# Attention, then a Gelu MLP, on one core: the first product of the MLP by seven block products from the fifth tile on, and high halves split by ScalarE

## Chip, cores and metric

One NeuronCore of a Trainium2 chip runs the whole program. The metric is the device time of one execution in microseconds (us); lower is better. Engines are named as the profile names them: PE is TensorE (PEld its weight loads), DVE is VectorE, ACT is ScalarE, POOL is GpSimd, SP issues DMAs.

## What is computed

```python
# q, k, v: 8 batches x 8 heads x 576 x 64, float32
scores = q @ k.T / sqrt(64)                      # causal, window of 128, ALiBi bias
attn   = exp(scores - max) / (sum + 1e-9)
x      = (attn @ v)   reshaped to 4608 x 512     # heads side by side
h      = x @ w_in                                # 512 -> 2048
out    = (0.5 * h * (1 + erf(h / sqrt(2)))) @ w_out   # 2048 -> 512
```

## The kernel before

The 4608 rows of x are cut into nine tiles of 512 tokens (t = 0 to 8). A batch has 576 tokens, so the attention of batch b fills the rest of tile b and the start of tile b + 1. Heads are worked in pairs; a pair of one batch is a *unit*, four units a batch.

Numbers of float32 precision are kept as two float16 halves: a *high part*, the value times a power of two, rounded, and a *low part*, what rounding left (`low_part`, L145, one VectorE instruction that reads the value and the high part). A product of two such numbers is three float16 matmuls: high by high, low by high, high by low. Batch 0 and half of tile 0 are in plain float32.

Tile by tile, from t = 1 on, the loop at L767 does 32 steps. Steps 0 to 15 are `mlp_in` (L588): 12 matmuls of 512 columns for one 128-wide slice of h, then Gelu by ScalarE out of PSUM into a float32 tile (L618), the high part of g by POOL (L619), the low part by VectorE (L620, a line of the helper L146). Steps 16 to 31 are `mlp_out` (L638): 12 matmuls of 512 columns each, and after every fourth step an eviction (`ob`, L661 by ScalarE or L663 by VectorE) and a store. Beside tile t stand the units of batch b = t + 1: `scores` (matmuls L410, scaled and biased into SBUF by VectorE, L432), `softmax` (row maxima L502, exp by ScalarE L505, z, the high part of e by ScalarE for b < 3 and by POOL from batch 3 on (L512, L514), the low part by VectorE, a transpose by DMA), and `weigh` (matmuls L554; the result goes to x by ScalarE L567 and VectorE). Their steps are in a table: scores at 2, 11, 16, 21, weigh at 12, 20, 25, 30 (other ones for t = 1). Once a tile, `split_v` and `split_qk` (L328, L350) measure and split the next batch's v, q and k in whole, 2560 and 2304 elements a partition.

PSUM has four banks for the MLP ("mm") and four for attention ("att"). x has two buffers, the float32 rooms "ob" three; each weight slice of w_in stays in SBUF, split into halves (`wi`). One e tile, `e_main`, serves all units. A scheduler orders the instructions of each engine from the order of the code, priorities and its own estimates; on the chip each engine keeps that order.

## Time and profile before

| | |
|---|---|
| median of 3 runs | 950.54 us (947.49 to 952.1) |
| the profiled execution | 956.14 us, of which its span (first to last instruction) is 954.3 |
| mean granted TensorE clock | 0.984 |
| busy in the span | PE 920.4, DVE 626.1, ACT 493.4, POOL 214.5 us |
| start of tile 2, 4, 7, 8 | 288.26, 492.50, 784.79, 867.67 us |
| last matmul ends | 950.56 us |

A group of instructions reads: line, engine, operation, out <- in, shapes, count | busy us, mean ns of one | idle time of the engine before them and who ended it. A row of the windows gives a stretch of the span, its length, the busy time of each engine with its number of instructions, the granted clock, the share of the DMA engines and GB/s. Matmuls overlap, so the mean of one (381 ns) is longer than the distance from one to the next. The kernel is compiled to lines of its own; line numbers below are those of the kernel before, unless they are said to be of the changed one.

### The profile page before, as it was taken

What the parts mean: (1) busy time and instruction counts of PE and PEld (TensorE: products, weight loads), DVE (VectorE), ACT (ScalarE), POOL (GpSimd) and SP (SyncE); (2) the same over time, 40 slices, a digit from 0 to 9 for tenths busy, and PEclk for the clock granted to TensorE, in tenths of its full rate; (3) what the DMA queues carried; (4) which work ended last, traced back from release to release, by engine and by line L of the source; (5) the groups of instructions that cost most, each with busy time, mean ns of one, the idle gap of its engine ahead of it and who ended that gap; (6) DMA issues with size and microseconds to landing.
All of it is one profiled execution on the core that took longest, in us unless ns stands there. A gap on an engine that the chain in (4) does not pass through costs nothing.

```text
span 954.3 us, 17680 instructions
## 1 busy us (share of the span) xinstructions
PE 920.4 (96%) x7068; PEld 448.8 (47%) x7068; DVE 626.1 (66%) x1270; ACT 493.4 (52%) x1071; POOL 214.5 (22%) x444
## 2 busy tenths in 40 slices
PE   7979999889999899999999999999999999999998
PEld 3554444544544444444544454444544454444443
DVE  6799989689786877497768876777566722201200
ACT  5978967767653664366525653564366313101200
POOL 1010000023001542053314430353044312201200
PEclk9889999799999999999999999999999999999999
DMA  9517433961473226522472346144312430000000
GB/s 313 211 65 264 179 105 94 208 191 29 98 176 99 50 58 144 148 46 55 77 201 46 56 94 178 52 77 94 73 30 50 92 75 1 1 23 23 1 12 33
DMA packets 172450, 91.18 MB, mean 96 GB/s; under 512 B 132560, under 2 KB 153168, under 8 KB 172240
## 3 DMA queue, kind: packets, MB, share of 16 engines
q1 hardware_dynamic: 172368, 90.06, 37.7%
q8 instruction: 55, 0.90, 0.4%
q14 instruction: 27, 0.22, 0.1%
HBM read 46.53 MB, written 9.44 MB: 59 GB/s over the span
## 4 chain that ended last, share of the span: by engine, by line
PE 54%; DMA 2%; DVE 2%; ACT 2%; issue 1%; SPq 0%; POOL 0%; DVEq 0%
PE o L653 26%; PE h L595 22%; PE av L554 3%; PE sc L410 2%; DMA v<-vp 1%; DMA q<-qp 1%; DVE stv L214 1%; DMA et<-e_main 1%; ACT vbuf L332 1%; DVE vbuf L146 0%; ACT s L505 0%; DVE kbuf L146 0%; ACT L618 0%; ACT L505 0%; SPq L305 0%
## 5 line engine op out<-in xcount | busy, mean ns | idle before, releaser
L595 PE MATMUL h<-x,wi 128*128 128x512 f16 x1728 | 385.0, 381 | 6.6 <-ACT g L618 3.0
L653 PE MATMUL o<-wo,g 128*128 128x512 f16 x1224 | 276.4, 379 | 0.2 <-DVE wo L146 0.2
L595 PEld LDWEIGHTS <-wi 128*128 128x128 f16 x1728 | 166.8, 98 | 209.2 <-issue 12.3
L653 PEld LDWEIGHTS <-g 128*128 128x128 f16 x1632 | 155.0, 98 | 186.6 <-issue 2.3
L146 DVE SCALAR_TENSOR_TENSOR g<-g,sg,g 128x512 f16<-128x512 f32 (+1 forms) x144 | 114.1, 805 | 92.7 <-POOL g L619 91.5
L619 POOL TENSOR_SCALAR g<-g,sg 128x512 f16<-128x512 f32 x128 | 100.4, 788 | 316.7 <-ACT g L618 312.4
L505 ACT ACTIVATE s<-s,nmax 128x192 f32<-128x192 f32 x252 | 111.2, 442 | 103.2 <-DVE nmax L502 103.0
L618 ACT ACTIVATE g<-h,gs 128x512 f32<-128x512 f32 x128 | 85.9, 687 | 135.8 <-PE h L595 111.0
L146 DVE SCALAR_TENSOR_TENSOR e_main<-s,z,e_main 128x192 f16<-128x192 f32 x252 | 107.3, 468 | 15.0 <-POOL e_main L514 10.2
L514 POOL TENSOR_SCALAR e_main<-s,z 128x192 f16<-128x192 f32 x180 | 87.1, 503 | 84.9 <-ACT s L505 29.3
L653 PE MATMUL o<-wo_first,g 128*128 128x512 f16 x408 | 94.6, 382 | 2.8 <-DMA wo_first<-wo 2.8
L410 PE MATMUL sc<-kbuf,qbuf 64*64 64x192 f16 (+1 forms) x1656 | 75.6, 264 | 10.8 <-DMA kbuf<-kp 4.5
L432 DVE SCALAR_TENSOR_TENSOR s<-sc,cs,bias_h 128x384 f32<-128x384 f32 x112 | 63.7, 606 | 14.3 <-PE sc L410 14.1
L567 ACT ACTIVATE x<-av,cx 128x448 f16<-128x448 f32 (+6 forms) x52 | 23.7, 474 | 72.8 <-PE av L554 72.6
L437 POOL MEMSET s<- 64x128 f32 (+1 forms) x112 | 19.2, 172 | 185.8 <-DVE s L432 167.3
L502 DVE TENSOR_REDUCE nmax<-s 128x5 f32<-128x960 f32 (+1 forms) x56 | 58.4, 1044 | 2.1
L661 ACT ACTIVATE ob<-o,so 128x512 f32<-128x512 f32 x17 | 11.5, 678 | 91.2 <-PE o L653 91.1
L410 PEld LDWEIGHTS <-qbuf 64*64 64x64 f16 x1512 | 36.1, 106 | 43.0 <-issue 40.2
L663 DVE TENSOR_SCALAR ob<-o,so 128x512 f32<-128x512 f32 x17 | 12.6, 744 | 60.0 <-PE o L653 60.0
L554 PEld LDWEIGHTS <-vbuf 128*64 128x64 f16 x1680 | 43.3, 115 | 12.4 <-issue 11.5
L554 PE MATMUL av<-et,vbuf 128*64 128x128 f16 (+1 forms) x1680 | 46.4, 216 | 2.6 <-DMA et<-e_main 2.6
L505 ACT ACTIVATION_READ_ACCUMULATOR s<-s,nmax 128x1 f32 x252 | 47.1, 187 | 0.0
(139 smaller groups left out, 737.8 us busy)
## 6 DMA issues: line engine op xcount, KB each, us to landing
v<-vp SPq DMA_DIRECT2D x32, 320.0 KB, 5.1
out<-ob SPq DMA_DIRECT2D x36, 256.0 KB, 2.1
raw<-w_in SPq DMA_DIRECT2D x8, 1024.0 KB, 14.2
raw<-w_out SPq DMA_DIRECT2D x8, 1024.0 KB, 5.3
q<-qp SPq DMA_DIRECT2D x7, 1152.0 KB, 6.2
k<-kp SPq DMA_DIRECT2D x7, 1152.0 KB, 7.1
qbuf<-qp SPq DMA_DIRECT2D x4, 288.0 KB, 5.1
kbuf<-kp SPq DMA_DIRECT2D x4, 288.0 KB, 5.5
```

The costliest lines, as they stand in the source:

```text
L146: nc.vector.scalar_tensor_tensor(out=dst, in0=src, scalar=scale, in1=high, op0=ALU.mult, op1=ALU.subtract)
L410: nc.tensor.matmul(ps[bank][o, n, 0:W], a, m, start=(i == 0), stop=(i == len(terms) - 1 and b > 0), skip_group_check=True,)
L432: nc.vector.scalar_tensor_tensor(out=s[:, bank[0] : bank[0] + k, :], in0=ps[bank][:, 0:k, 0:W], scalar=cs, in1=bias.broadcast_to([P, k, W] ...
L502: nc.vector.tensor_reduce(out=nmax[:, r], in_=s[:, r], axis=AX.X, op=ALU.max, negate=True)
L505: nc.scalar.activation(s[:, i, :], s[:, i, :], AF.Exp, bias=nmax[:, i : i + 1], accum_out=z[:, i : i + 1])
L514: nc.gpsimd.tensor_scalar(e[:, i, 0, c], s[:, i], z[:, i : i + 1], 1.0, op0=ALU.mult, op1=ALU.mult)
L554: nc.tensor.matmul(av[r, (j - blocks[0]) * QB : (j - blocks[0] + len(js)) * QB], v32s[b][:, hp, kb, r] if b < EXACT else vbuf[:, vi, hp, k ...
L567: nc.scalar.activation(x[:, 0], av[:, :n], AF.Copy, scale=c)
L595: nc.tensor.matmul(ph, wi[n][:, a, cc, k * P : (k + 1) * P], x[:, cc, b, :], start=(i == 0), stop=(i == 3 * NCC - 1),)
L618: nc.scalar.activation(g32, ph, AF.Gelu, scale=gsc[t, n])
L619: nc.gpsimd.tensor_scalar(g[:, r, 0], g32, gsg[t, n], 1.0, op0=ALU.mult, op1=ALU.mult)
L653: nc.tensor.matmul(o, both[:, a, c], wo[n][:, b, k, :], start=(fc == first and i == 0), stop=(fc == last and i == 2),)
```

## The change

1. **Seven products.** For tiles 4 to 8 (`FAST = 4`), `mlp_in` is replaced by a class `Seven`. For a quarter d of the 2048 columns of h (512 columns), x and w_in are taken as 2 x 2 blocks (halves of the tokens by alternate 128-row slices of the 512, and halves of the columns by those slices), and the block product is formed from seven products in place of eight, after Strassen and Winograd. A product is 12 matmuls of 256 columns, two slices of 256 side by side in one PSUM bank. Two banks are held a quarter, u and v. The products gather in them, and partial results are copied out (s1, s2, s3, by ScalarE) and added to v by VectorE. Each of the four results then has Gelu, its high part (ScalarE) and its low part (VectorE).

```python
def add(self, ps, w, m, first):
    n = 0
    for k in range(2):
        for i in range(2):
            for a, b in ((0, 0), (1, 0), (0, 1)):
                nc.tensor.matmul(
                    ps[:, k * HT : (k + 1) * HT], w(a, i)[:, k * P : (k + 1) * P], m(b, i),
                    start=first and n == 0, stop=True, skip_group_check=True,
                )
                n += 1

def out(self, hi, tok, src, room=None):
    ...
    room = src if room is None else room
    nc.scalar.activation(room, src, AF.Gelu, scale=gsc[t, 2 * d])
    ...
    nc.scalar.activation(g[:, :, 0], v, AF.Copy, scale=gsg[t, 2 * d])
    low_part(g[:, :, 1], v, gsg[t, 2 * d], g[:, :, 0])

p1: u  = lo0 . x1           ; s1 = copy(u)
p2: v  = lo1 . x2           ; s1 = v + s1 ; out(s1)
p6: u += T2 . S2            ; s2 = copy(u)
p5: v  = hi0 . S1
p7: u += T3 . S3            ; s3 = copy(u) ; s3 = v + s3 ; out(s3)
p4: u += T4 . x2'           ; out(u)
p3: v += hi1 . S4           ; s2 = v + s2 ; out(s2)
```

The last seven lines are the seven methods in short. `seven_steps` puts them in the order p1 p2 p6 p5 p7 for the first quarter, p1 p2 p4' p6 p3' p5 p7 for the next ones (' is of the quarter before), 13 steps of two products; the last p4 and p3 stand in the first steps of `mlp_out`. The tile then has 29 steps.

2. **Sums of weights**, `sums_of_weights`, beside tiles 2 and 3 (steps 4, 8, 12 and 16): eight times two VectorE sums of 512 elements, four of 256, a high part of 1024 by ScalarE and a low part by VectorE, and four stores to DRAM. T1 takes the place of weights in SBUF; T2, T3 and T4 are streamed back, 256 KB for a quarter and a tile (60 loads in all).

3. **Sums of x**, `sums_of_x`, twice for each of tiles 4 to 8, when the units that fill them have been weighed: VectorE sums of 1024 and four times 256, a high part by ScalarE, a low part by VectorE.

4. **High parts by ScalarE** everywhere: POOL's two instructions are gone.

```diff
-                if st.b < 3:
-                    nc.scalar.activation(e[:, i, 0, c], s[:, i], AF.Copy, scale=z[:, i : i + 1])
-                    continue
-                nc.gpsimd.tensor_scalar(e[:, i, 0, c], s[:, i], z[:, i : i + 1], 1.0, op0=ALU.mult, op1=ALU.mult)
+                nc.scalar.activation(e[:, i, 0, c], s[:, i], AF.Copy, scale=z[:, i : i + 1])
...
-        nc.gpsimd.tensor_scalar(g[:, r, 0], g32, gsg[t, n], 1.0, op0=ALU.mult, op1=ALU.mult)
+        nc.scalar.activation(g[:, r, 0], g32, AF.Copy, scale=gsg[t, n])
```

5. **q and k from batch 4 on** come pair by pair, twice: `load_pair` and `measure` for the maxima, then `load_pair` and `split_pair` (576 elements a partition) before the scores. Batches 3 on hold two pairs' halves in the space of four. v, q and k of a batch get their scales together (`scales`).

6. **The table of steps.** A fast tile runs scores of units 1, 2 and 3 at steps 4, 8 and 15, of unit 0 of the next batch at 22, weigh at 14, 19, 22, 25. Softmax of units 1 and 2 is held back to step 14, behind the seven products, with a gate. Unit 0 of batch 5 moves into tile 3 (step 25). Row maxima (`maxima`) are taken before the exps of the whole unit.

```diff
-    SCORES_AT, WEIGH_AT = (2, 11, 16, 21), (12, 20, 25, 30)
+    AT = ((8, 14, 18, 22), (17, 22, 26, 30)), ((2, 11, 16, 21), (12, 20, 25, 30)), ((4, 8, 15), (14, 19, 22, 25))
```

7. Buffers: one tile `ldbuf` with two halves takes the place of the rotating "ld" buffers; the sums of x, the streams and two rooms for s2 lie in it from tile 4 on. Weights of w_in share a scale in pairs of slices. A few powers of two follow.

What the order becomes, at three places. TensorE, the first product of tile 8, before: two slices of h follow each other, each in a bank of its own (h8_0, h8_1).

```order
L595 MATMUL h8_0_10073<-x8_8835,wi0_679 128x512
L595 LDWEIGHTS wi0_679
L595 MATMUL h8_0_10073<-x8_8835,wi0_679 128x512
L595 LDWEIGHTS wi0_679
L595 MATMUL h8_1_10091<-x8_8835,wi0_679 128x512 [waits Activation_49]
```

And now: the end of p7 and the start of p4 of the first quarter, both in bank u8_0, where p4 waits for ScalarE's copy of p7's result.

```order
L816 MATMUL u8_0_10947<-ldbuf_77 128x256
L816 LDWEIGHTS ldbuf_77 [waits DMAHW7_49]
L816 MATMUL u8_0_10947<-x8_9756,ldbuf_77 128x256 [waits Activation_49]
L816 LDWEIGHTS ldbuf_77
L816 MATMUL u8_0_10947<-x8_9756,ldbuf_77 128x256
```

The matmuls are 256 columns wide, and the next one in the order needs the bank of the last.

ScalarE at the same place, before: one Gelu after the other, each from the next bank (g32 is the float32 room, h8_n the bank).

```order
L618 ACTIVATE g32_8_0_10087<-h8_0_10073,gs8_0_10067 128x512 [waits DMAHW6_49,PE_49,Activation_49]
L618 ACTIVATE g32_8_1_10104<-h8_1_10091,gs8_0_10067 128x512 [waits DVE_49,DMAHW7_49,PE_49,Pool_49]
L618 ACTIVATE g32_8_2_10121<-h8_2_10108,gs8_0_10067 128x512 [waits DMAHW0_49,PE_49,Activation_49]
L618 ACTIVATE g32_8_3_10138<-h8_3_10125,gs8_0_10067 128x512 [waits DVE_49,PE_49]
L618 ACTIVATE g32_8_4_10156<-h8_4_10142,gs8_0_10067 128x512 [waits DVE_49,PE_49]
```

And now: copies (s1, s3, s2 in ldbuf), Gelus and high parts (g8) of two quarters in turn.

```order
L837 COPY s18_0_10960<-u8_0_10947 128x512 [waits DMAHW1_49,PE_49,Activation_49]
L827 ACTIVATE s18_0_10960<-s18_0_10960,gs8_10937 128x512 [waits DVE_49]
L830 ACTIVATE g8_0_10943<-s18_0_10960,sg8_10938 128x2x256 [waits Activation_49]
L848 COPY ldbuf_77<-u8_0_10947 128x512 [waits PE_49]
L856 COPY s38_0_11017<-u8_0_10947 128x512 [waits DMAHW2_49,PE_49]
L837 COPY s18_1_11037<-u8_1_11024 128x512 [waits DMAHW3_49]
L827 ACTIVATE s38_0_11017<-s38_0_11017,gs8_10937 128x512 [waits DVE_49]
L827 ACTIVATE s18_1_11037<-s18_1_11037,gs8_10937 128x512 [waits DVE_49]
L827 ACTIVATE s48_0_11068<-u8_0_10947,gs8_10937 128x512 [waits PE_49,Activation_49]
```

Nine instructions of ScalarE now stand where two slices of h had two, and most of them wait for VectorE, TensorE or ScalarE itself.

VectorE early in tile 2, before: low parts of g and what the units need.

```order
L146 SCALAR_TENSOR_TENSOR g2_0_3381<-g32_2_0_3382,sg2_0_3364,g2_0_3381 128x512 [waits Pool_49]
L146 SCALAR_TENSOR_TENSOR g2_0_3381<-g32_2_1_3399,sg2_0_3364,g2_0_3381 128x512 [waits Pool_49]
L432 SCALAR_TENSOR_TENSOR s3_0_3431<-sc3_0_0_3432,cs3_3145,bias_h_61 128x384 [waits PE_49]
L432 SCALAR_TENSOR_TENSOR s3_0_3431<-sc3_0_2_3433,cs3_3145,bias_h_61 128x384 [waits PE_49]
L146 SCALAR_TENSOR_TENSOR g2_0_3381<-g32_2_2_3427,sg2_0_3364,g2_0_3381 128x512 [waits Pool_49]
L214 TENSOR_REDUCE stv4_3607<-v32_4_3405 128x1 [waits DMAHW5_49,DMAHW6_49,DMAHW4_49,DMAHW3_49]
```

And now, near the same place (ldbuf from wi are the sums of weights, sta5 and stb4 measures of the next batches, kbuf and qbuf the split of a pair).

```order
L150 SCALAR_TENSOR_TENSOR g2_1_3479<-g32_2_4_3480,sg2_3340,g2_1_3479 128x512 [waits Activation_49]
L150 SCALAR_TENSOR_TENSOR kbuf_83<-qbuf_82,scb3_2375,kbuf_83 128x576 [waits Activation_49]
L150 SCALAR_TENSOR_TENSOR qbuf_82<-qbuf_82,scb3_2375 128x576 [waits Activation_49]
L763 TENSOR_TENSOR ldbuf_77<-wi2_709 128x512 [waits DVE_49]
L763 TENSOR_TENSOR ldbuf_77<-wi3_712 128x512
L121 TENSOR_REDUCE square_75<-quarters_3678 32x3 [waits DVE_49]
L228 TENSOR_REDUCE sta5_4771<-kbuf_83 128x2 [waits DMAHW6_49,DMAHW5_49]
L150 SCALAR_TENSOR_TENSOR g2_1_3479<-g32_2_5_3580,sg2_3340,g2_1_3479 128x512 [waits Activation_49]
```

The scheduler has put the sums of weights ahead of the steps where the code has them: 18 of their 56 VectorE instructions stand before the first low part of g of tile 2, 38 between it and tile 3, none later.

## Prediction

> **What bounds the kernel now.** I read the windows by tile first (one row per tile of 512 tokens, cut where the first matmul of a tile starts; tiles 2 to 8), then the chain of waits at the end.

> ```profile
> core 0: us, PE busy (x) PEld busy (x) DVE busy (x) ACT busy (x) POOL busy (x), PEclk, DMA share, GB/s
> 288.26:391.74 103.48, 100.36 (x919) 48.72 (x918) 74.78 (x151) 52.65 (x113) 32.95 (x68) 0.98 0.42 94
> 391.74:492.50 100.76, 99.05 (x818) 47.55 (x817) 74.28 (x150) 51.05 (x112) 32.90 (x68) 0.98 0.42 95
> 492.50:590.26 97.76, 97.15 (x865) 46.95 (x864) 74.05 (x150) 51.53 (x112) 32.37 (x68) 1.00 0.44 98
> 590.26:687.72 97.46, 97.46 (x817) 47.11 (x816) 70.20 (x150) 53.06 (x113) 33.13 (x68) 1.00 0.35 74
> 687.72:784.79 97.07, 97.07 (x842) 46.90 (x841) 57.85 (x111) 45.48 (x109) 32.57 (x68) 1.00 0.30 61
> 784.79:867.67 82.88, 82.88 (x385) 37.55 (x384) 13.74 (x19) 13.65 (x19) 11.20 (x16) 1.00 0.04 13
> 867.67:950.56 82.89, 82.88 (x384) 37.40 (x382) 13.52 (x18) 12.37 (x18) 11.12 (x16) 1.00 0.04 13
> ```

> ```profile
> 784.79 41.44 PE h L595 x192
> 826.23 41.44 PE o L653 x192
> 867.67 41.44 PE h L595 x192
> 909.11 41.45 PE o L653 x192
> 950.56 0.02 issue
> 950.59 0.69 ACT ob L661
> ```

> TensorE is never idle from tile 5 on, and within 0.6 us of that in tile 4. The last two tiles are nothing but two blocks of 192 matmuls, each 41.44 us, or 215.8 ns a matmul of 512 columns. So in the tiles that the change rebuilds, time saved on TensorE is time saved, as long as no other engine takes its place; VectorE is busy for 70 to 75 us and ScalarE for 51 to 53 us of a tile of 97 us. Tile 2 takes 103.48 us where tile 6 takes 97.07 with the same matmuls: 6.4 us there are waits and a lower granted clock (0.98), a measure of what late VectorE and ScalarE work can cost a tile here. Tile 3 loses 3.7 us in the same way, tile 4 loses 0.7.

> **TensorE: fewer columns.** From tile 4 on, the 192 matmuls of L595 become 4 quarters x 7 products x 12 = 336 matmuls of 256 columns. Matmuls of that width with full weights do not occur before, so their price is bounded. Half of 215.8 ns, 107.9, is the floor. The other end comes from the start of the program, where a matmul of 192 columns is followed by one with other weights:

> ```profile
> 28.61 0.26 PE L422 MATMUL sc<-bias_h,adders 128*128 128x192 bf16 x1
> 28.70 0.19 PE L422 MATMUL sc<-adders 128*128 128x64 bf16 x1
> ...
> 28.60 0.11 PEld L422 LDWEIGHTS <-adders 128*128 128x128 bf16 x2 [0.28 <-issue]
> ```

> The second starts 90 ns after the first. A straight line through 192 columns (90 ns) and 512 (215.8) gives 115 ns at 256. I take 110, nearer to the floor, since rows of 10 ns are coarse and the floor comes from 192 matmuls in one piece. Then a first product takes 336 x 0.110 = 37.0 us in place of 41.44: 4.5 us saved a tile, **22.4 us over five tiles**. The ends are 36.3 us (5.2 a tile, 26 in all) and 38.7 us (2.7 a tile, 14 in all). All the rest of TensorE's work stays.

> Each matmul still loads 128x128 weights, now for half the columns, and this is where the change could fail outright:

> ```profile
> L595 PE MATMUL h<-x,wi 128*128 128x512 f16 x1728 | 385.0, 381 | 6.6 <-ACT g L618 3.0 <-ACT ob L661 2.1 <-ACT g L612 1.1
> L595 PEld LDWEIGHTS <-wi 128*128 128x128 f16 x1728 | 166.8, 98 | 209.2 <-issue 12.3
> ```

> A load lasts 98 ns. If it stood between matmuls, a matmul of 512 columns would come every 300 ns or so; it comes every 215.8 ns, so the load is hidden, and the 90 ns above leave no room for 98 ns beside 192 columns either. [...]

> **ScalarE and VectorE: what is added.** High parts move from POOL to ScalarE, and each quarter of a fast tile adds three copies out of PSUM, three sums on VectorE, and the sums of x. The nearest prices:

> ```profile
> L618 ACT ACTIVATE g<-h,gs 128x512 f32<-128x512 f32 x128 | 85.9, 687 | 135.8 <-PE h L595 111.0 <-DVE g L146 22.2 <-issue 1.6
> L619 POOL TENSOR_SCALAR g<-g,sg 128x512 f16<-128x512 f32 x128 | 100.4, 788 | 316.7 <-ACT g L618 312.4 <-DVE s L432 4.3
> L614 ACT ACTIVATE g<-g,sg 128x256 f16<-128x256 f32 x16 | 8.2, 539 | 0.1
> L204 ACT ACTIVATE wi<-zi,sww 128x1024 f16<-128x1024 f32 x8 | 8.7, 1139 | 2.4 <-DVE sww L141 2.4
> L512 ACT ACTIVATE e_main<-s,z 128x192 f16<-128x192 f32 x72 | 26.5, 442 | 9.4 <-DMA et<-e_main 4.3 <-DVE z L509 2.0 <-issue 1.6
> L493 ACT COPY et<-tp 128x512 f32<-128x512 f32 x16 | 9.0, 614 | 1.6 <-PE tp L491 1.6
> L663 DVE TENSOR_SCALAR ob<-o,so 128x512 f32<-128x512 f32 x17 | 12.6, 744 | 60.0 <-PE o L653 60.0
> L146 DVE SCALAR_TENSOR_TENSOR g<-g,sg,g 128x256 f16<-128x256 f32 x16 | 7.4, 478 | 1.1 <-ACT g L614 1.1
> L193 DVE SCALAR_TENSOR_TENSOR zi<-zi,raw 128x1024 int32<-128x1024 int32 x8 | 9.7, 1219 | 0.0
> L332 ACT ACTIVATE vbuf<-v,scv 128x2560 f16<-128x2560 f32 x7 | 17.1, 2439 | 0.8 <-PE av L554 0.7
> L146 DVE SCALAR_TENSOR_TENSOR vbuf<-v,scv,vbuf 128x2560 f16<-128x2560 f32 x7 | 20.2, 2881 | 10.4 <-ACT vbuf L332 10.4
> L432 DVE SCALAR_TENSOR_TENSOR s<-sc,cs,bias_h 128x384 f32<-128x384 f32 x112 | 63.7, 606 | 14.3 <-PE sc L410 14.1
> L502 DVE TENSOR_REDUCE nmax<-s 128x5 f32<-128x960 f32 x28 | 32.2, 1151 | 2.0
> ```

> A high part of 512 elements lies between 539 ns (256) and 1139 ns (1024); 0.7 us is taken. In tiles 1 to 3 ScalarE then gains 16 x 0.7 = 11 us for g and, where POOL split e before (tiles 2 and 3), 36 x 0.442 = 16 us: 51 + 27 = 78 us of 100, still with slack, so nothing is charged. With POOL silent, VectorE speeds up; its low parts of g by tile:

> ```profile
> 288.26:391.74 103.48, 14.01 (x16) 0.98 0.42 94
> 784.79:867.67 82.88, 12.03 (x16) 1.00 0.04 13
> ```

> That is 876 ns each beside POOL's e work and 752 without: 2 us a tile for g. [...]

> Sums of weights: 8 sets of two of 512 elements (0.744), four of 256 (0.478) and one of 1024 (1.219), 4.6 us each, 37 us in all. By the built order 18 of the 56 stand before the first low part of tile 2 and 38 between there and tile 3: about 25 us on VectorE in tile 2. 74.8 + 25 - 2 = 98 of 103 us by durations, less by pace, since instructions start before the last has ended (three L146 of 468 ns mean take 1.06 us together):

> ```profile
> 653.54 1.06 DVE L146 SCALAR_TENSOR_TENSOR e_main<-s,z,e_main 128x192 f16<-128x192 f32 x3
> ```

> Their cover is those 29 us of idle VectorE. It is thin, so I charge 1 us (0 to 6, the loss of tile 2 now).

> The first product of tiles 4 to 6, on VectorE: 12 sums x 0.744 + 16 low parts x 0.752 + two units of scores (4 x 0.606 + 0.41 each, 5.7) + their maxima (1.15 + 0.94 each, 4.2) + v's maximum (2.8) + four split halves of 576 (3) + about 20 small ones (3) = 39.6 us, beside 37.0 + 3.2 us of TensorE. VectorE is as full as TensorE there, and a bank of PSUM returns to TensorE only after a VectorE sum or a ScalarE copy. I charge **2.5 us a tile, 7.5 in all**; the ends are 0 (by pace VectorE has a tenth to spare) and 6.4 us (tile 2 now).

> Tile 4's start: its sums of x hang on the last unit weighed in tile 3. From there, in VectorE's and ScalarE's built order: x (0.5 and 0.5), a sum of 1024 (1.2), two of 256 (1.0), v's low part (2.9), one more (0.5), x of tile 5 (0.5), the sum s1 (0.7), the last of 256 (0.5), Gelu (0.7), the high part (1.1) and the low part (1.2): 11.3 us. TensorE has about 9 us in that time (the end of tile 3, three products, one unit of scores). **2 us** (0 to 4).

> Tiles 7 and 8: 12 copies x 0.614 + 32 x 0.7 = 30 us of ScalarE in 37, 21 us of VectorE. The built order puts p7 and p4 of quarter 0 next to each other on one bank, with a copy of 0.61 us between: 0.8 us a tile with the hand-overs, **1.6 us**. In tiles 4 to 6 scores stand there instead. Streams of weights (256 KB, reloaded every 9 us) and the second reading of q and k lie under transfers that now land in 5 to 7 us; nothing is charged. The first 288 us keep their work: 0, give or take 2. Afterwards the end is the same eviction of 0.69 us.

> **Sum.** -22.4 + 1 + 7.5 + 2 + 1.6 = -10.3 us. The profiled execution took 956.14 us (span 954.3 and 1.8 around it), 5.6 above the median 950.54; the sum comes off both: 945.8 for one like it, **940.2, say 940 us**, for the median.

> **Rivals.** *The waits are next to nothing.* Pace rather than duration rules VectorE, the relief from POOL pays for the sums of weights, and the floor of 107.9 ns holds: -26 + 1.6 is 926 us. For it: VectorE's rows overlap. Against: tiles 2 and 3 lose 6.4 and 3.7 us now at VectorE 74 of 100.

> *The gain is eaten.* Each fast tile with attention loses 6 us to the chain TensorE, copy, sum, Gelu on engines that keep their order, and the start 4: -22.4 + 18 + 4 + 2 = +1.6, about 952 us. For it: VectorE's 39.6 us beside 40.

> *Slower: VectorE becomes the bound.* If it runs at its durations plus its waits, tiles 1 and 2 pay 4 and 6 us for the sums of weights and tiles 4 to 6 pay 7 each, with 115 ns a matmul: -14 + 10 + 21 + 4 + 2 = +23, 973 us; at 110 ns 965. It decides from the point where VectorE's waits exceed a tenth of the stage, since pace leaves about a tenth. Against it: in tile 4 VectorE works 74 of 98 us and TensorE loses 0.7.

> *Weight loads stand bare.* 107.9 + 98 = 206 ns x 336 = 69 us a product, +28 a tile, 1088 us. [...]

> That the halves are not built at all is excluded: the order shows the 256-column matmuls.

> **How the numbers follow.** Forecast 0.50, no waits 0.17, eaten 0.18, VectorE bound 0.13, bare loads 0.02. About 0.5% (4.8 us) is what a measurement of this kernel can tell from no change. Faster takes 0.46 of the forecast (its waits may come out 6 us larger, hence 0.04 for same), all of the second, and 0.02 of the third: 0.65. Same is 0.04 + 0.14 = 0.18; slower 0.02 + 0.15 = 0.17. The range goes from the second case to the upper side of the third: 925 to 957.

> **What would show it.** Windows by tile: tiles 7 and 8 near 79.2 us (41.44 + 37.0 + 0.8), tiles 5 and 6 near 95.5, tile 2 within 2 us of 103.5. In the tile of the slowest stage, waits of TensorE on ScalarE's copies and VectorE's sums of 2 to 3 us. I am wrong if the first product of tile 8 takes over 39 us (price of 256 columns), if tiles 4 to 6 show no gain (VectorE as the bound), or if tiles 1 to 3 grow by more than 4 us in all.

## The result, and the profile after

The changed kernel takes 983.98 us (median) against 951.32 us of the kernel before on the same chip: a ratio of 1.0343, 95% interval 1.0296 to 1.039. It is slower by 3.4% where 940 us were forecast. One of its four runs took 1736.61 us at a granted clock of 0.879 and is left out of the ratio; the other three took 982.91 to 984.39. The profiled execution took 984.39 us, its span 982.3. The changed kernel's windows, cut as those of before, with the two stretches ahead of tile 2:

```profile
core 0: us, PE busy (x) PEld busy (x) DVE busy (x) ACT busy (x) POOL busy (x), PEclk, DMA share, GB/s
0.00:196.68 196.68, 165.92 (x1236) 86.11 (x1237) 165.05 (x362) 149.83 (x333) 13.22 (x40) 0.97 0.59 175
196.68:296.33 99.65, 97.14 (x865) 47.15 (x865) 81.43 (x166) 71.44 (x165) 2.95 (x17) 0.98 0.57 133
296.33:408.77 112.44, 100.36 (x865) 49.21 (x864) 97.40 (x196) 80.26 (x176) 2.74 (x16) 0.97 0.66 168
408.77:519.66 110.89, 101.59 (x871) 48.72 (x870) 82.33 (x174) 85.24 (x200) 3.42 (x20) 0.98 0.56 130
519.66:625.04 105.38, 98.65 (x1010) 64.75 (x1009) 80.24 (x162) 74.22 (x176) 3.09 (x18) 0.95 0.49 116
625.04:724.41 99.37, 94.43 (x961) 61.67 (x960) 78.81 (x167) 72.58 (x173) 3.06 (x18) 1.00 0.54 128
724.41:820.56 96.15, 93.71 (x932) 61.09 (x931) 64.93 (x131) 62.26 (x146) 2.37 (x14) 0.98 0.44 94
820.56:899.51 78.95, 78.28 (x529) 51.66 (x528) 25.58 (x38) 32.42 (x49) 0.00 (x0) 1.00 0.18 54
899.51:978.62 79.11, 78.44 (x529) 51.56 (x527) 20.99 (x30) 29.35 (x46) 0.00 (x0) 1.00 0.13 44
```

Against before, in us: +8.1 up to tile 2 (296.33 for 288.26), then +9.0, +10.1, +7.6, +1.9, -0.9, -3.9, -3.8 for tiles 2 to 8; together +28.1. The two last tiles do what was forecast. The loss lies at and before tile 4, most of it where TensorE's work is almost what it was. From tile 2 on TensorE idles for 36.8 us (the lengths of the rows less PE's busy time), against 5.5 in the kernel before. Whom it waits for, from 195 us on (total, count and longest), before and then in the changed kernel:

```profile
PE h L595 <- ACT g L618: 3.0, 2, 2.4
PE sc L410 <- DVE s L432: 1.7, 1, 1.7
```

```profile
PE sc L484 <- DVE s L506: 11.7, 7, 3.0
PE av L631 <- DMA et<-e_main: 7.9, 5, 2.3
PE h L674 <- ACT g L697: 4.1, 3, 2.3
```

So TensorE now waits most for VectorE's evictions of scores and for the transposes of e, which follow the softmax; the waits for Gelu have hardly grown.

The price of the narrow matmuls, from the changed kernel's timeline of TensorE at the start of tile 8 (start, length, engine, line, operation, count):

```profile
899.51 1.47 PE L816 MATMUL u<-x,wi 128*128 128x256 f16 x12
900.82 1.47 PE L816 MATMUL v<-x,wi 128*128 128x256 f16 x12
902.13 1.47 PE L816 MATMUL u<-x,wi 128*128 128x256 f16 x12
...
909.52 1.47 PE L816 MATMUL u<-x,ldbuf 128*128 128x256 f16 x12 [0.67 <-ACT s L856]
```

Products of twelve start 1.31 us apart: 109 ns a matmul, with a weight load of 98 ns (mean of the 960 of L816 from wi) for each, which is thus hidden. The last row is p4 of quarter 0 waiting 0.67 us for the copy.

Early in tile 4 the same kernel shows what the rest costs. VectorE first, then TensorE, then the windows:

```profile
531.66 2.82 DVE L228 TENSOR_REDUCE stb<-v 128x1 f32<-128x2560 f32 x1 [2.50 <-issue]
534.40 1.13 DVE L506 SCALAR_TENSOR_TENSOR s<-sc,cs,bias_h 128x384 f32<-128x384 f32 x2
```

```profile
535.06 1.92 PE L484 MATMUL sc<-kbuf,qbuf 64*64 64x192 f16 x33 [3.04 <-DVE s L506]
536.91 2.74 PE L816 MATMUL u<-x,ldbuf 128*128 128x256 f16 x12
```

```profile
530.00:540.00 10.00, 6.96 (x69) 5.15 (x67) 8.26 (x15) 2.93 (x6) 0.68 (x4) 0.73 0.20 54
540.00:550.00 10.00, 10.00 (x99) 7.84 (x98) 9.41 (x18) 7.38 (x13) 0.40 (x2) 0.93 0.43 139
```

The maximum of the next batch's v stands in VectorE's order ahead of the scores' evictions, starts 2.50 us after the instruction before it (the profile names no releaser; its chain of waits has the load of v ahead of it, landed at 529.49, and then 2.18 us that it cannot name; in a kernel below it names the load of v) and takes 2.82 us; TensorE waits 3.04 us for a bank; and the product behind the wait takes 2.74 us where 1.47 is usual, at a granted clock of 0.50 (0.73 over these 10 us). So this wait is paid twice, as 3.04 us of idle time and again as slower matmuls.

### The profile page after: what moved, and what is told of

Same layout as the page of the kernel before. It is cut to its first block, busy times and chain, and to the rows that moved or that the text cites. A ratio compares the mean times of both kernels' runs of the same rounds, so it can differ in the third digit from the quotient of the medians.

```text
span 982.3 us, 19642 instructions
## 1 busy us (share of the span) xinstructions
PE 908.5 (92%) x7788; PEld 521.9 (53%) x7788; DVE 696.8 (71%) x1419; ACT 658.3 (67%) x1461; POOL 30.8 (3%) x143
## 4 chain that ended last, share of the span: by engine, by line
PE 39%; ACT 5%; DMA 3%; DVE 2%; issue 1%; SPq 0%; ACTq 0%
PE o L732 18%; PE u L816 11%; PE v L816 8%; ACT s L585 3%; DMA et<-e_main 2%; PE av L631 2%; PE sc L484 1%; ACT e_main L591 1%; DVE e_main L150 1%; DMA v<-vp 0%; ACT L585 0%; DMA ldbuf<-stored 0%; DVE stb L228 0%; DVE s L506 0%; ACT ldbuf L827 0%
## 5 line engine op out<-in xcount | busy, mean ns | idle before, releaser
L674 PE MATMUL h<-x,wi 128*128 128x512 f16 x768 | 175.8, 387 | 10.6 <-ACT g L697 4.1
L585 ACT ACTIVATE s<-s,nmax 128x192 f32<-128x192 f32 x252 | 110.9, 441 | 41.9 <-DVE nmax L572 41.8
L591 ACT ACTIVATE e_main<-s,z 128x192 f16<-128x192 f32 x252 | 92.1, 441 | 25.5 <-DMA et<-e_main 18.6
L484 PE MATMUL sc<-kbuf,qbuf 64*64 64x192 f16 (+1 forms) x1656 | 81.2, 268 | 24.0 <-DVE s L506 12.2
L816 PEld LDWEIGHTS <-wi 128*128 128x128 f16 x960 | 93.4, 98 | 12.7
L150 DVE SCALAR_TENSOR_TENSOR e_main<-s,z,e_main 128x192 f16<-128x192 f32 x252 | 90.7, 412 | 11.0 <-ACT e_main L591 10.8
L816 PEld LDWEIGHTS <-ldbuf 128*128 128x128 f16 x720 | 69.7, 99 | 17.5 <-issue 2.7
L484 PEld LDWEIGHTS <-qbuf 64*64 64x64 f16 x1512 | 39.8, 108 | 48.2 <-issue 45.5
L816 PE MATMUL u<-ldbuf 128*128 128x256 f16 x480 | 60.5, 275 | 2.2 <-DMA ldbuf<-stored 1.5
L150 DVE SCALAR_TENSOR_TENSOR g<-s,sg,g 128x512 f16<-128x512 f32 x60 | 44.1, 745 | 23.9 <-ACT g L830 23.8
L816 PE MATMUL v<-ldbuf,wi 128*128 128x256 f16 x480 | 57.0, 273 | 0.0
L150 DVE SCALAR_TENSOR_TENSOR g<-g,sg,g 128x512 f16<-128x512 f32 (+1 forms) x64 | 42.1, 678 | 8.8 <-ACT g L698 4.6
```

The source lines that it names most:

```text
L150: nc.vector.scalar_tensor_tensor(out=dst, in0=src, scalar=scale, in1=high, op0=ALU.mult, op1=ALU.subtract)
L484: nc.tensor.matmul(ps[bank][o, n, 0:W], a, m, start=(i == 0), stop=(i == len(terms) - 1 and b > 0), skip_group_check=True,)
L585: nc.scalar.activation(s[:, i, :], s[:, i, :], AF.Exp, bias=nmax[:, i : i + 1], accum_out=z[:, i : i + 1])
L591: nc.scalar.activation(e[:, i, 0, c], s[:, i], AF.Copy, scale=z[:, i : i + 1])
L674: nc.tensor.matmul(ph, wi[n][:, a, cc, k * P : (k + 1) * P], x[:, cc, b, :], start=(i == 0), stop=(i == 3 * NCC - 1),)
L816: nc.tensor.matmul(ps[:, k * HT : (k + 1) * HT], w(a, i)[:, k * P : (k + 1) * P], m(b, i),  start=first and n == 0, stop=True, skip_group_ ...
```

## The experiments

The theories. A: the sums of weights fill VectorE in tiles 1 to 3. B: ScalarE is late with the high parts that GpSimd had. C: q and k by pairs, with measures of the next batch that stand on loads in VectorE's order. D: the held-back softmax comes as a burst in tile 4. Tile lengths in us, cut at each tile's first matmul, and medians; the ratio is to the kernel before on the same chip. The row of the kernel before comes from an execution of 956.14 us, 4.8 above the median, while the other rows come from executions within 1.8 us of theirs; in the last kernel of this document, whose order on ScalarE is that of before up to tile 7, tile 3 takes 97.0 us and not 100.8. So a loss read off the rows for tile 3 may be up to 4 us too small. (Tile 6 of the kernel before is cut as in its row above, 0.17 us after the first matmul of tile 7.)

| kernel | start of 2 | 2 | 3 | 4 | 5 | 6 | median | ratio |
|---|---|---|---|---|---|---|---|---|
| before | 288.3 | 103.5 | 100.8 | 97.8 | 97.5 | 97.1 | 951.3 | 1 |
| g's high parts on ScalarE | 288.9 | 101.4 | 97.5 | 97.1 | 97.6 | 96.9 | 951.8 | 0.9987 |
| e's high parts on ScalarE | 288.7 | 104.5 | 99.2 | 99.6 | 99.7 | 96.9 | 960.0 | 1.0072 |
| both on ScalarE | 289.7 | 105.8 | 101.2 | 102.7 | 102.7 | 98.7 | 971.3 | 1.0214 |
| pairs alone | 292.3 | 109.9 | 104.6 | 98.0 | 97.7 | 96.9 | 970.9 | 1.0212 |
| no fast tile | 298.6 | 112.5 | 106.4 | 105.3 | 105.7 | 102.9 | 1002.1 | 1.0539 |
| no fast tile, measures late | 297.8 | 104.3 | 108.0 | 104.1 | 104.9 | 102.8 | 992.4 | 1.0409 |
| the changed kernel | 296.3 | 112.4 | 110.9 | 105.4 | 99.4 | 96.2 | 984.0 | 1.0343 |
| ... GpSimd's high parts back | 291.0 | 114.0 | 117.0 | 103.8 | 104.0 | 91.4 | 986.1 | 1.0361 |
| ... no sums | 297.7 | 113.5 | 108.3 | 104.2 | 101.9 | 96.2 | 984.8 | 1.0336 |
| ... GpSimd back, no sums | 294.5 | 113.0 | 113.4 | 102.0 | 103.1 | 91.7 | 979.5 | 1.0287 |
| ... measures late | 296.9 | 113.1 | 114.2 | 100.4 | 100.9 | 96.4 | 986.5 | 1.0351 |
| ... measures late, no sums | 295.6 | 104.4 | 116.8 | 101.1 | 100.0 | 96.5 | 978.5 | 1.0271 |
| ... and e on GpSimd | 295.0 | 107.0 | 116.2 | 100.1 | 96.3 | 91.8 | 968.8 | 1.0167 |
| ... and the unit in tile 4 | 291.7 | 104.8 | 117.0 | 105.7 | 96.1 | 91.4 | 970.3 | 1.0210 |
| ... not held back | 298.9 | 111.1 | 110.7 | 117.3 | 115.9 | 105.5 | 1023.5 | 1.0732 |

### The parts by themselves

**Both high parts**, in the kernel before:

```diff
-                nc.gpsimd.tensor_scalar(e[:, i, 0, c], s[:, i], z[:, i : i + 1], 1.0, op0=ALU.mult, op1=ALU.mult)
+                nc.scalar.activation(e[:, i, 0, c], s[:, i], AF.Copy, scale=z[:, i : i + 1])
...
-        nc.gpsimd.tensor_scalar(g[:, r, 0], g32, gsg[t, n], 1.0, op0=ALU.mult, op1=ALU.mult)
+        nc.scalar.activation(g[:, r, 0], g32, AF.Copy, scale=gsg[t, n])
```

> The kernel before, with one part of the change alone: the high parts of g and e go to ScalarE. Theory A (the sums of weights overfill VectorE in tiles 1 to 3) expects no cost: 947 to 954 us, tiles 2 and 3 near 103.5 and 100.8. Theory B (ScalarE, with the high parts that GpSimd had, comes late with Gelu and the exps) expects most of the loss here: 968 to 985 us, tiles 2 and 3 longer by 8 to 10 us each and TensorE waiting there for ScalarE's Gelu and for s, whose two buffers come free after the softmax. Theory C (q and k by pairs, twice) expects 947 to 954, as A.

971.29 us, ratio 1.0214 (1.0172 to 1.0256): B holds in total, but the loss is spread over tiles 2 to 6, with 5 us in each of tiles 4 and 5, and not 8 to 10 us in each of tiles 2 and 3. TensorE's waits for Gelu grow from 3.0 to 10.8 us and those for evictions of scores from 1.7 to 5.7. VectorE's 151 instructions in tile 2 do get shorter, with GpSimd busy there for 2.77 us in place of 32.95: 69.99 us for 74.78. **One half each:**

> The kernel before with half of the first experiment: only e's high parts go to ScalarE (180 of 442 ns, 80 us), g's stay on GpSimd. Both together cost 20 us. If the cost comes from the work as such, shared by busy time: 959 to 963 us. If g's high parts do it, since each stands between two Gelus that TensorE waits for: 950 to 955. If e's do it: 966 to 971.

> The kernel before with the other half of the first experiment: only g's high parts go to ScalarE (128 of 718 ns, 92 us), e's stay as they were. Both together cost 20 us, e's alone 7 to 9. If the two add up: 962 to 965. If either alone is nearly free and the sum is not (waits that pass the length at which TensorE's clock falls only when both are there): 952 to 958.

With e's alone 960.03 us, 1.0072 (1.0049 to 1.0095); with g's alone 951.82, 0.9987 (0.9972 to 1.0001). The 92 us of g's high parts cost nothing by themselves, the 80 us of e's 7 us, the two together 20. Busy time on ScalarE prices none of this; where the place in its order shows is early in tile 2, with e's alone (ScalarE, then TensorE):

```profile
318.31 0.19 ACT L505 ACTIVATION_READ_ACCUMULATOR s<-s,nmax 128x1 f32 x1
318.40 1.82 ACT L511 ACTIVATE e_main<-s,z 128x192 f16<-128x192 f32 x5
320.24 1.28 ACT L615 ACT_TABLE_LOAD   x1
321.53 0.69 ACT L615 ACTIVATE g<-h,gs 128x512 f32<-128x512 f32 x1
```

```profile
322.27 4.90 PE L592 MATMUL h<-x,wi 128*128 128x512 f16 x16 [4.04 <-ACT g L615]
```

and TensorE in the kernel before:

```profile
320.32 4.03 PE L595 MATMUL h<-x,wi 128*128 128x512 f16 x11 [2.42 <-ACT g L618]
```

Five high parts stand between the exps and the Gelu that returns a bank; TensorE waits 4.04 us there, 2.42 in the kernel before. Why both halves together cost more than the sum of each is not shown further.

**Pairs alone, and no fast tile:**

```diff
-FAST = 4
+FAST = 99
```

> No fast tile, and GpSimd makes the high parts as before: of the change there are left q and k by pairs with their measures, the common scales and the maxima ahead of the exps. Two causes are in play now: B, the high parts on ScalarE (20 us by themselves in the kernel before), and C, the measures and pairs, which stand early in VectorE's order and wait there for loads, with the scores' evictions queued behind them. If the two add up, C is what the run without a fast tile lost over the run with the high parts alone, 31 us: 978 to 986 us. If C only costs where ScalarE is full as well: 951 to 960.

> The changed kernel with no fast tile (FAST = 99): eight block products everywhere, no sums of weights or of x, no softmax held back; high parts on ScalarE, maxima ahead of the exps and q and k by pairs stay. A: 950 to 960 us. B: all nine tiles carry ScalarE's high parts, 975 to 1000. C: 965 to 985, and the loss sits in tiles 3 to 6, where pairs are loaded, and not in tile 2's first half.

The first also has GpSimd's instructions back, and keeps what else is left of the change: common scales, maxima ahead of the exps, the one buffer. It takes 970.93 us, 1.0212 (1.0168 to 1.0256): between the two cases foreseen, 19 us, and in the profile all of its loss lies ahead of tile 4. With ScalarE's high parts as well it is 1002.12 us, 1.0539 (1.05 to 1.0578): 20 and 19 make 51, twelve more than their sum. The profiles tell of what kind the excess is: from 195 us to the last matmul TensorE idles 7.8 us before, 17.3 with both high parts on ScalarE, 16.8 with pairs alone and 39.1 with both, which is 12.8 more than the two add up to. At half clock (last section) it is busy for 6.5, 12.5, 14.2 and 22.3 us, half of which is lost, and that adds 1 us more. So the fast tiles, which this kernel lacks, are worth 18 us to the changed one, their sums and the held-back softmax paid for. A falls as the whole cause: there are no sums of weights here, and tile 2 takes 112.5 us. Its place, VectorE, TensorE and windows in turn:

```profile
313.83 2.82 DVE L228 TENSOR_REDUCE stb<-v 128x1 f32<-128x2560 f32 x1 [2.89 <-DMA v<-vp]
316.56 1.13 DVE L506 SCALAR_TENSOR_TENSOR s<-sc,cs,bias_h 128x384 f32<-128x384 f32 x2
```

```profile
317.22 0.69 PE L484 MATMUL sc<-kbuf,qbuf 64*64 64x192 f16 x23 [4.08 <-DVE s L506]
317.84 17.40 PE L674 MATMUL h<-x,wi 128*128 128x512 f16 x72
```

```profile
313.00:317.20 4.20, 0.15 (x1) 0.00 (x0) 3.37 (x3) 1.40 (x2) 0.00 (x0) 1.00 0.33 117
317.20:335.20 18.00, 17.98 (x95) 7.92 (x95) 16.73 (x46) 15.34 (x34) 0.68 (x4) 0.91 0.37 119
```

VectorE stands on the load of v for 2.89 us and reads it for 2.82, with two evictions behind. The 72 matmuls after the wait take 17.40 us; 72 x 215.8 ns are 15.5, and the clock is 0.91. **The same with the measures late**, each load of a pair let go by a low part of this tile, the maximum of v too:

```diff
+            nc.gpsimd.tensor_copy(src32[n][:, 0, 0:1], gate)
...
-                if step == 9:
-                    scales(b + 1)
+                if step == 10:
+                    stat_v(b + 1, g_of[t, 1][:, 3, 1, 0:1])
+                if step == 16:
+                    scales(b + 1)
```

> The run without a fast tile again (1002 us), with the measures moved: loads of q and k for measuring are let go by a copy on GpSimd from the low part of g of steps 0, 4, 8 and 12, the maximum of v by one of step 7, so that VectorE's order has them behind the evictions of the first unit's scores. C: the waits of 4 us in tile 2 and their like go, 980 to 992 us. If the place of the measures doesn't matter: 998 to 1005.

992.40 us, 1.0409 (1.0381 to 1.0437), 0.4 above the range that C gave: tile 2 falls from 112.5 to 104.3. C is shown for tile 2; tile 3 gets 1.6 us longer.

### One cause at a time taken from the changed kernel

**GpSimd's high parts back** (the first diff the other way); **no sums of weights:**

```diff
-        for m in range(2):
-            w = wi[2 * d + m]
...
-            nc.sync.dma_start(stored[n, d, :, :, i], st[:, :, k])
+            nc.sync.dma_start(stored[n, d, :, :, i], wi[2 * d + m][:, :, 2 * i + c])
```

> The changed kernel with that one part undone: GpSimd makes the high parts of g in tiles 1 to 3 and those of e from batch 3 on, as before. A: GpSimd's instructions slow VectorE down and nothing else improves, 982 to 990 us. B: 957 to 966 us, tiles 2 and 3 back to 103 to 105 us each. C: 982 to 988.

> The changed kernel without the arithmetic of the sums of weights: the 32 stores to DRAM take slices of the weights themselves, so 56 instructions of VectorE (37 us by their durations) and 8 of ScalarE are left out, while stores, streams and the seven products stay, with wrong numbers in them. A: tiles 1 to 3 lose their 3.4, 9.0 and 10.1 us again, 960 to 967 us. B: ScalarE is as late as ever, 978 to 985. C: the same 978 to 985.

> The changed kernel with GpSimd's high parts back and without the arithmetic of the sums of weights (56 instructions of VectorE and 8 of ScalarE left out; the products get wrong numbers). Each edit alone moved nothing. If each only covered the other (with the sums VectorE had 102 us to do in tile 2 once GpSimd slowed it): 958 to 968 us, tile 2 near 104. If what is late is neither (theory C, the measures): 978 to 986, and tile 2 still 110 or more.

The runs without sums store slices of the weights themselves. 986.12 us (1.0333 to 1.039), 984.80 (1.0296 to 1.0376) and, with both edits, 979.49 (1.0254 to 1.032). Without the sums VectorE's work in tile 2 falls from 97.40 to 75.38 us and the tile is no shorter:

```profile
297.73:411.21 113.48, 101.78 (x866) 48.79 (x864) 75.38 (x152) 76.01 (x171) 2.76 (x16) 0.94 0.53 131
```

By these three runs alone, next to nothing would be left of A and B. **Measures late, then also no sums, then also e's high parts on GpSimd:**

> The changed kernel, seven products and all, with only the measures moved behind: loads of q and k for measuring let go by low parts of g in tiles 2 and 3, the maximum of v gated there and in the fast tiles. Theory C (VectorE stands on a load of v or q and k with the scores' evictions queued behind it): TensorE's wait of 3.0 us early in tile 4 and the slow clock after it go, and some of tile 2's, 970 to 978 us. If the waits only come back behind other instructions: 982 to 986.

> The changed kernel with measures late, as in the run of 986 us, and also without the arithmetic of the sums of weights (left out as before; wrong numbers in the products). Each of the two edits alone moved nothing. If each cause alone is enough to make VectorE late in tiles 2 and 3, taking both away must show: tile 2 from 113 to 104 to 106, 970 to 976 us. If the loss moves on once more (to e's high parts on ScalarE): 980 to 986.

> The same with e's high parts back on GpSimd from batch 3 on; g's stay on ScalarE, where they alone cost nothing. If the three causes together are the loss: tile 2 near 103, tile 3 under 106, 952 to 964 us, near the forecast again. If something else keeps tiles 2 to 5 slow: above 968.

Measures late alone: 986.49 us (1.033 to 1.0372). This is outside the 970 to 978 us that C gave: tile 4 gains the 5 us of its wait and slow clock, but tile 3 loses 3 and tile 2 is unchanged. Without sums as well, 978.48 us (1.0233 to 1.031): now tile 2 falls by 8.7, while tile 3 loses 2.5. The windows of tile 2 in these two kernels, and of tile 3 in the second:

```profile
296.91:409.97 113.06, 101.07 (x866) 49.63 (x865) 92.32 (x202) 78.87 (x175) 4.74 (x20) 0.97 0.57 145
```

```profile
295.55:399.92 104.37, 97.86 (x865) 47.27 (x864) 71.15 (x161) 72.83 (x168) 3.56 (x20) 1.00 0.49 114
399.92:516.67 116.75, 104.99 (x871) 50.21 (x870) 91.82 (x195) 82.05 (x197) 4.24 (x24) 0.94 0.60 154
```

So in tile 2 the early measures and the sums are each enough to make it 113 us; one has to take away both to see either. With e on GpSimd too, 968.82 us (1.0118 to 1.0216), above the 952 to 964 expected: tiles 5 and 6 fall below the kernel before (96.3 and 91.8 us), but tile 3 stays at 116. **The moved unit back in tile 4:**

```diff
+        if t == FAST:
+            scores_at, weigh_at = (1, 4, 8, 15), (11, 19, 22, 25)
```

> The run of 969 us with the order of units of the kernel before: unit 0 of batch 5 is scored in tile 4 (step 1, softmax at once, weighed at step 11), not at the end of tile 3. If that unit, with the split of its pair, is what made tile 3 take 116 us: tile 3 at 106 or less, 956 to 963 us, tile 4 a few us longer than 100. If tile 3 is slow for the sums of x or the pairs: still 112 or more, 966 to 975.

970.31 us (1.0175 to 1.0244); tile 3 is still 117, tile 4 5.6 us longer. The moved unit is not it. What is left in tile 3 and not in the kernel before are the sums of x, pairs split beside it, and stores and streams; which of them costs 16 us or more stays open. The rows narrow it down: with late measures and both high parts on ScalarE, tile 3 takes 108.0 us without a fast tile and 116.8 with fast tiles and no sums of weights. So about half of the loss needs no fast tile, and 9 us come with them.

**Not held back:**

```diff
-                    if fast and step <= len(first):
-                        waiting.append(st)
-                    else:
-                        softmax(st)
+                    softmax(st)
```

> The changed kernel with one thing undone: the softmax of units 1 and 2 of a fast tile runs as soon as their scores are there, not behind the seven products. If the burst of held-back exps is what tile 4 loses (theory D): 974 to 980 us, tile 4 from 105.5 to 98 or so. If holding it back keeps the copies of the seven products prompt: 986 to 995, with TensorE waiting in the seven products for ScalarE's copies and VectorE's sums.

1023.49 us, 1.0732 (1.0706 to 1.0759). That is 28 us above the second case. D falls: the burst is the cheaper way. With exps in between, TensorE waits in the seven products for the copies (whole waits, count and longest, from tile 4 to 6):

```profile
PE u L816 <- ACT s L856: 15.1, 5, 6.3
PE u L816 <- ACT ldbuf L848: 6.3, 3, 5.3
```

### Versions meant to be faster

Parts of before everywhere (GpSimd, q and k whole), seven products where attention is gone or nearly so:

> A version meant to beat both: GpSimd's high parts, q, k and v whole and measured as before, seven products in tiles 7 and 8 alone, all eight sums of weights beside tile 6, where VectorE works 58 us of 97. Tiles 7 and 8 gain 3.9 us each, so 943 to 946 us if the sums are hidden; 948 to 953 if 37 us more of VectorE in tile 6 make TensorE wait there.

> Seven products in tiles 7 and 8 as in the run of 957 us, whose tile 6 lost 10 us with all sums of weights early in it; here one set goes to the end of tile 5 and the others are let go one by one through tile 6 by a copy on GpSimd. If the loss came from their crowding ahead of scores and low parts: tile 6 within 3 us of 97, 944 to 948 us. If VectorE has no room for 32 us more there wherever they stand: 953 to 958.

> Parts of before everywhere, seven products in tile 8 alone, its sums of weights beside tile 7, where VectorE works 14 us of 83 and no attention is left. Each earlier run has 3.9 us of gain in tile 8 and nothing here can make TensorE wait: 946 to 949 us. If something of the change that is left (scales shared by pairs of slices, one buffer for q and k, maxima first) costs time early: 950 to 953.

```diff
-FAST = 4
+FAST = 7
...
-    SUMS_AT = (4, 8, 12, 16)
+    SUMS_AT = (1, 4, 8, 10, 15, 18, 24, 28)
```

957.22 us, 1.0058 (1.0036 to 1.008): tiles 7 and 8 take 79.0 and 79.1 us, tile 6 with all the sums 107.1. Spread out, 955.91 us, 1.0031 (1.0014 to 1.0048), tile 6 104.4. The first is above both of its cases, the second within the worse of its two. The sums do cost 7 to 10 us there, which is what two fast tiles bring. With only tile 8 fast and its sums beside tile 7, 952.32 us, 0.9996 (0.9977 to 1.0015): tile 8 gains its 3.8 us, and tile 2 starts 4.2 us later than before, 3.6 of them from tile 0's first product (from first h to first o 48.2 us for 44.6).

**The order of tile 0 kept.** The same put into the kernel before, with its buffers and its maxima, and no gate added ahead of tile 7; the maximum over two slices, for their common scale, is taken into an instruction that was there, and the sums are gated into tile 7. ScalarE's order is then the old one up to tile 7:

```diff
-        over_partitions(stat, len(ns), True, STAT_FLOOR)
+        nc.gpsimd.partition_all_reduce(stat, stat, P, bass_isa.ReduceOp.max)
+        nc.vector.scalar_tensor_tensor(
+            out=stat[:, 0:1], in0=stat[:, 0:1], scalar=STAT_FLOOR, in1=stat[:, 1:2], op0=ALU.max, op1=ALU.max
+        )
```

> Seven products in tile 8 alone, put into the kernel before in such a way that ScalarE's order is the old one, instruction for instruction, up to tile 7 (the common scale of two weight slices comes from an instruction that was there already; buffers as before). The run of 952 us with the same tile 8 had another order in tile 0 and its tile 2 started 4 us later. If that order was where its 3.9 us went: 946 to 949 us. If tile 8's gain is lost elsewhere: 950 to 953.

948.11 us, 0.995 (0.9932 to 0.9968): half a per cent faster than the kernel before, and faster than the changed one. Tile 0's first product takes 45.1 us (44.6 before); tiles 7 and 8:

```profile
780.04:862.92 82.88, 82.88 (x386) 37.59 (x385) 51.88 (x81) 23.90 (x29) 17.38 (x24) 1.00 0.29 86
862.92:942.03 79.11, 78.44 (x529) 51.58 (x527) 21.01 (x30) 29.34 (x46) 0.00 (x0) 1.00 0.14 44
```

## Why the prediction was wrong, point by point

The forecast was -10.3 us and the measured change +32.7, or +28.1 between the profiled executions. Stage by stage, forecast and measured: up to tile 2, 0 and +8.1; tiles 2 and 3, +1 and +19.1; tile 4, 0 and +7.6; tiles 5 and 6, -4 and +1.0; tiles 7 and 8, -7.4 and -7.7. The saving on TensorE was right; what failed are the terms for late work on ScalarE and VectorE, two of them put at nothing.

- **TensorE, -22.4 us: right in price.** 110 ns were taken, 109 measured; tiles 7 and 8 were to take 79.2 us and take 78.95 and 79.11, the wait of p4 included (0.8 forecast, 0.67 measured). Against the same kernel without fast tiles, tiles 5 and 6 save 6.3 and 6.7 us, more than the 4.5 forecast, in part because the kernel without fast tiles has four waits of 1.6 to 4.5 us there and matmuls 1.7 us slower in all behind each of two of them. The rival of bare weight loads is out: 206 ns a matmul were its price, and with a load of 98 ns for each they come 109 ns apart.
- **"ScalarE then gains 27 us ... nothing is charged": the step that failed first.** It read slack from a tile's mean (78 of 100). The cost by itself, in the kernel before, is 20 us, most of it waits of TensorE for Gelu and for evictions of scores (10.8 and 5.7 us for 3.0 and 1.7). In the changed kernel it is covered by other losses: taken away alone, it gains nothing (986.1 for 984.0 us); with late measures and no sums, e's part alone is worth 9.7 us.
- **"The second reading of q and k ... nothing is charged": the second.** The transfers were counted, the measures that wait for them on VectorE were not. With the split by pairs and the smaller edits they cost 19 us by themselves; moving the measures gives back 8 us in tile 2 of the kernel without fast tiles and 5 in tile 4 of the changed one.
- **Sums of weights, +1 (0 to 6).** Below 1 beside the other losses, 8.7 us in tile 2 once the measures are late, 7 to 10 in tile 6. The 29 us of idle VectorE that were named as cover took in only part: with the measures late, the sums bring 21 us of busy time to tile 2 (92.32 for 71.15) and 8.7 of them come out as time.
- **Tiles 4 to 6, 2.5 us each, and tile 4's start, 2.** Tile 4 comes out 7.6 us above its forecast (105.4 for 97.8 - 4.5 + 2.5 + 2 = 97.8): two waits of 3.0 us, one for VectorE's evictions and one, by the profile, for the low parts of e, and a low clock behind each (0.50 for 6.83 and for 3.41 us, 0.95 over the tile, some 5 us). With measures late it is 100.4.
- **"The first 288 us: 0 +- 2".** +8.1. Tile 0's first product is 3.4 us longer, and tile 1 is 5.1 us longer from first matmul to first matmul. The instructions added there are small, but they moved the order of all engines; the version that keeps ScalarE's order has tile 0 back at 45.1 us. Which of the edits there moves it was not taken apart; with GpSimd's high parts back, tile 2 starts at 291.0, 5.3 us earlier.
- **Left out of the sum altogether: the clock.** The prediction saw 0.98 in tile 2 and took it for part of "6.4 us"; the clock was low behind some long waits and not behind others (last section). From tile 2 on TensorE is busy at half clock for 21.2 us in the changed kernel and for 6.5 before, which is 7.4 us lost. It is not why 20 and 19 us make 51: there it adds 1 us. Nor are the 6.4 us all waits and clock, as it read them: tile 2 has 77 more matmuls than tile 6 (919 for 842), 3.1 us of idle TensorE and one stretch of 3.4 us at half clock. The 3.7 us of tile 3 are for the most part one wait of 1.7 us and the clock of 0.50 for 3.41 us behind it.

Of the tests that the prediction named, tile 8 passes, "tiles 1 to 3 grow by more than 4 us in all" is met five times over, and tiles 4 to 6 show no gain (300.9 us for 292.3). The rival "VectorE becomes the bound" had the sign and, within 11 us, the time. Its 25 us for tiles 4 to 6 and the start of tile 4 are near the measured 22 (12.1, 6.4 and 3.6 us above the price of TensorE alone), but ahead of tile 4 it had 10 us for 27, so that the total is in part luck. Its reason is half right: TensorE does wait for VectorE most (11.7 us for evictions of scores), but not for VectorE's busy time as such, since taking 22 us of that from tile 2 left the tile as long as it was.

## What to carry to other kernels

The slack in the mean of a tile (ScalarE was busy for 52.65 of the 103.48 us of tile 2) was not there for the taking in the fixed order of these engines: both high parts on ScalarE cost 20 us. Price an added instruction by what stands behind it in that order and who waits for that, and an instruction that waits for a load also by the time until the load lands. When undoing one suspect moves nothing, undo two: several causes may each be enough for the same wait. A gain at the end of the program, where no attention is left, was had for its full price (3.9 and 3.8 us in tiles 7 and 8); taken in tile 8 alone, it reached the median (948.11 us) where ScalarE's order up to tile 7 was left as it was.

## What the runs showed of the hardware that was not expected

Some long waits of TensorE were followed by slower matmuls here, and others of the same length were not. In seven traces (before, and six kernels from the experiments, from 195 us on), none of 29 waits of 0.5 to 1.7 us, 5 of 14 between 1.7 and 2.4 and 12 of 14 between 2.4 and 4.5 were followed by 512-column matmuls that took 0.8 to 2.2 us longer in all than 215.8 ns each; 1.7 us is the commonest.

Two waits of the same length, in the kernel with both high parts on ScalarE, show the difference:

```profile
426.54 5.34 PE L592 MATMUL h<-x,wi 128*128 128x512 f16 x24 [2.04 <-ACT g L615]
630.30 7.03 PE L592 MATMUL h<-x,wi 128*128 128x512 f16 x24 [2.04 <-ACT g L615]
```

```profile
422.58:425.99 3.41, 1.92 (x9) 0.78 (x8) 2.44 (x7) 3.38 (x8) 0.00 (x0) 1.00 0.00 0
425.99:429.41 3.42, 2.87 (x14) 1.33 (x14) 1.78 (x5) 3.42 (x8) 0.00 (x0) 1.00 0.98 182
627.38:630.79 3.41, 1.37 (x8) 0.54 (x6) 1.74 (x6) 3.38 (x7) 0.00 (x0) 1.00 0.17 35
630.79:634.21 3.42, 3.42 (x10) 1.24 (x9) 2.65 (x6) 3.39 (x8) 0.00 (x0) 0.50 1.10 204
```

The same at the wait of 2.42 us in the kernel before, and then at the wait of 3.04 us in the changed one:

```profile
316.56:319.97 3.41, 1.34 (x7) 0.49 (x5) 3.26 (x18) 3.38 (x10) 2.50 (x4) 1.00 0.00 0
319.97:323.39 3.42, 3.07 (x8) 1.12 (x8) 2.69 (x12) 2.14 (x4) 3.03 (x6) 0.50 0.79 150
323.39:326.80 3.41, 3.41 (x18) 1.49 (x16) 3.41 (x6) 0.61 (x1) 2.17 (x3) 1.00 0.40 77
```

```profile
531.12:534.53 3.41, 0.91 (x9) 0.67 (x7) 2.87 (x2) 1.07 (x2) 0.00 (x0) 1.00 0.39 138
534.53:537.94 3.41, 2.88 (x38) 2.29 (x38) 3.34 (x9) 1.44 (x2) 0.54 (x3) 0.50 0.00 0
537.94:541.36 3.42, 3.42 (x18) 2.35 (x16) 3.42 (x8) 1.67 (x3) 0.34 (x2) 0.50 0.13 22
541.36:544.77 3.41, 3.41 (x37) 2.79 (x36) 3.41 (x7) 2.55 (x5) 0.20 (x1) 1.00 0.68 224
```

Cut in this way, these two traces have 437 stretches at full clock. None of the 428 in which TensorE idled for at most 0.48 of the time was followed by one at 0.50, two of the four with 0.50 to 0.59 were, and so were all five with 0.60 to 0.87. Of the ten stretches at 0.50, the eight with at most 0.10 of idle time were followed by full clock, and the two with 0.16 and 0.55 were not. These are counts of two executions; what sets the clock is not shown.

A stretch of 3.41 us at 0.50 loses 1.7 us, the commonest excess above, and the product of 2.74 us for 1.47 stands in such stretches. TensorE was not idle throughout the stretch before: 1.34, 1.37 and 0.91 us of busy time stood there, and in the seven traces waits of 1.71 to 2.15 us were followed by slower matmuls in five cases.
